# Two-block attention on one core: the second block's exponentials taken for two heads at once, and one head's maxima over two chunks from the positive part of their difference

## The chip, the cores and the metric

The kernel runs on one core of a Trainium2 chip. The metric is device time in microseconds (us): the median of 3 runs is 1816.2 us, between 1811.39 and 1816.44. The trace that is read below is of one profiled execution of 1817.04 us, of which the recorded span of instructions takes 1815.3 us. The engines go by their names in the profile: PE is TensorE (PEld its loading of weights), DVE is VectorE, ACT is ScalarE, POOL is GpSimd, SP issues DMAs.

## What is computed

Two attention blocks, A and B, each with its own input of 2048 tokens by 512 features, 32 heads of 16 features, and its own output; the outputs stand side by side in the result. Block A has a sliding window of 256 tokens, block B is full attention, and it is block B that the change touches.

```python
def _B_ref(x, wqkv, wo):
    B, S, D = x.shape
    H = 32
    Dh = D // H
    qkv = transpose((x @ wqkv).reshape(B, S, 3, H, Dh), 2, 0, 3, 1, 4)
    q, k, v = qkv[0], qkv[1], qkv[2]
    scores = jnp.einsum("bhqd,bhkd->bhqk", q, k) * (Dh ** -0.5)
    p = _softmax(scores, axis=-1)
    o = jnp.einsum("bhqk,bhkd->bhqd", p, v)
    return transpose(o, 0, 2, 1, 3).reshape(B, S, D) @ wo
```

## The kernel before, in words

**Units and steps.** Heads go in groups of four (HG) and queries in chunks of 512 (QC). A unit is one group and one query chunk, so block B has 32 units. Within a unit, 16 steps run over the tiles of 128 keys. One step is, for its 128 keys and the unit's 512 queries: four score matmuls, one per head (`scores`, line 615; 51 rows of K as weights, Q as moving data), an exponential of each 128x512 result (line 622, ScalarE, PSUM to the SBUF tile `p`), and four products of values and exponentials (`weigh2`, line 646), which are issued two steps after their scores and accumulate in PSUM bank 0. A head's 16 features appear as 48 rows, since numbers are split into two parts; 3 further rows carry the negated row maximum, so the exponential sees scores with the maximum already taken off. The heads of a group sit at array rows 0 and 64 (`ROW`): two matmuls that stand next to each other with different halves run in the array at the same time. Here such a couple is called a pair.

**Maxima one unit ahead.** While a unit's steps run, the row maxima of the next unit are made: for each of four tiles of 128 queries and each of four chunks of 512 keys (16 items a unit), the four heads' scores are computed again the other way round (`max2`, line 458; Q as weights, K as moving data), and VectorE reduces them over the keys (line 462) into `mt`. GpSimd then joins the four chunks (`max_chunk`), and splits the result (`max_finish`). PE transposes it (`max_rows`, line 582), ScalarE copies it out, and two DMAs lay it into the 3 rows of Q.

**The order.** Engines work through their instructions in the order in which the code records them, and a semaphore holds an instruction until its data is there or its buffer is free. For block B the order is a string of letters that is walked through again and again. One walk is called a round here: it covers two steps and two items of maxima. Before, with `s` a score matmul and its exponential, `M` the maxima of heads 0 and 1 (one reduction over 128x1024), `m` that of one further head (a reduction over 128x512), and a digit so many quarters of a step's `weigh2`:

```python
ORDER = "ssm4mssMs2msms2sM"
```

The last 20 steps, for which no maxima are left, go by `LAST`, with six matmuls of the output projection after every second step. Eight times early in block B, two output projections of block A (24 matmuls) are put in at a `4`. `STEP` is the planner's own clock per step; it sets when loads and later work are put into the order.

**PSUM.** There are eight banks of 128x512 float32. In block B, before: bank 0 for the products, banks 1 to 3 in turn for scores, banks 4 and 5 as the pair that `M` uses, banks 6 and 7 in turn (`room`) for `m`.

Of the kernel before, what the change touches and what calls it, by code (L numbers as in the profile page):

```python
# [20 lines left out]
HG = 4  # L21
# [13 lines left out]
NEG = -1.0e30  # L35
SCALE = DH ** -0.5
AHEAD = 3
STEP = 2.45
PACE = 16 * STEP


ORDER = "ssm4mssMs2msms2sM"
LAST = "ssss4"
AHEADM = 4
QU = 2.4

# [96 lines left out]
def attention_kernel(ctx: ExitStack, tc: tile.TileContext, xT, wqk, wv, wo, out):  # L143
# [79 lines left out]
    def view(bank):  # L223
        pool, n = bank
        if pool == "u":
            return ps_all[:, n + 1]
        first, width = {"e": (1, 1), "o": (0, 1), "p": (4, 2), "s": (6, 1)}[pool]
        n = first + width * n
        return ps_all[:, n] if width == 1 else ps_all[:, n:n + 2]

# [12 lines left out]
    later = mone.bitcast(mybir.dt.uint16)  # L243
    junk = cst.tile([128, 256], BF16, name="junk")
    xt = [cst.tile([128, 2, 4, 2 * HG], F32, name=f"nm{i}") for i in range(2)]
    opk = [cst.tile([128, HG // 2, S], F32R, name=f"opk{i}") for i in range(2)]
    vt = [cst.tile([128, NT, VP + 16 * i], F32, name=f"vt{i}") for i in range(2)]
    vst = [cst.tile([128, H, VW], F32, name=f"vst{i}") for i in range(2)]
# [4 lines left out]
    def constants():  # L253
        make_identity(nc, ident)
        nc.gpsimd.memset(minus, -1.0)
        nc.gpsimd.memset(wmask, 0.0)
        nc.gpsimd.affine_select(out=wmask[:, 128:], in_=wmask[:, 128:], pattern=[[-1, 128]],
                                compare_op=ALU.is_ge, fill=NEG, base=0, channel_multiplier=1)
        nc.gpsimd.memset(mone, 1.0)
        nc.gpsimd.affine_select(out=mone, in_=mone, pattern=[[0, 2], [1, 128]], compare_op=ALU.is_ge,  # L260
                                fill=zero_fill, base=-1, channel_multiplier=-1)
        nc.vector.memset(ps_all[:, 0], 0.0)
        for v in vst:
            nc.gpsimd.memset(v, 1.0)
        for v in xt:
            nc.gpsimd.memset(v, 0.0)
        nc.gpsimd.memset(vt[1][:, :, VP:], 1.0)
# [166 lines left out]
    def maxima(b, g, c):  # L434

        if not b:
            if (b, g, c) not in mt:
                xt.reverse()
                mt[b, g, c] = xt[0]
            return mt[b, g, c].rearrange("p a s (r q) -> p a r q s", q=4)  # L440
        if (b, g, c) not in mt:
            m = sb.tile([128, NQC, HG, 4], F32, name=f"mt_{b}_{g}_{c}",
                        **(dict(tag="mte", bufs=1) if (b, g, c) == (1, 0, 0) else dict(tag="mt", bufs=3)))
            mt[b, g, c] = m.rearrange("p k h q -> p h q k")
        return mt[b, g, c]

# [124 lines left out]
    def max_rows(b, g, c):  # L571
        n = f"{b}_{g}_{c}"
        nm = parts["nm"].bitcast(BF16).rearrange("p a s (n u) -> p a (s n) u", u=2)[:, :, :, 1]
        if slot[0]:

            bank = M.take("e")
            ps = view(bank)
        else:
            bank, ps = room()
        ps = ps.bitcast(BF16)  # L580
        for a in range(2):
            nc.tensor.transpose(ps[32 * a:32 * a + 32, :128], nm[:, a], ident)
        nt = sb.tile([64, 128], F32, name=f"ntr_{n}", tag="ntr")
        op = nc.scalar.activation(nt, ps[:64, :128], AF.Copy)
        t = mark(op, M.run("ACT", 200, M.pe("c", 80)))
        release(bank, t)
        for a in range(2):
            ready["q", b, g, c] = M.dma(12, t)
            nc.sync.dma_start(opq[b, g, c][ROW[a] + KS:ROW[a] + KM].bitcast(F32).rearrange(
                "s r (q t) -> s (r q) t", t=128), nt[32 * a + 8:32 * a + 32])  # L590
# [14 lines left out]
    def scores(b, g, c, kt, j, heads=1, pieces=((),)):  # L605

        n = f"{b}_{g}_{c}_{kt}"
        pr, a0 = divmod(j, 2)
        banks = [M.take("e" if b else "u") for _ in range(heads)]
        ps = [view(bank) for bank in banks]  # L610
        w = QC if b else sum(x[3] for x in pieces)
        for k, col, q0, n1 in [(kt, 0, 0, QC)] if b else pieces:
            for x in range(heads):
                rows = slice(ROW[a0 + x], ROW[a0 + x] + KM)
                nc.tensor.matmul(ps[x][:, col:col + n1], opk2(g)[rows, pr, 128 * k:128 * k + 128],  # L615
                                 opq[b, g, c][rows, pr, q0:q0 + n1], start=True, stop=True)
            t = M.pe("h", 235 if b else 12 + n1 / 2.4, ready["q", b, g, c])
        if a0 == 0:
            pts[b, g, c, kt, pr] = sb.tile([128, 2, QC], F32, name=f"p_{n}_{pr}", tag="p", bufs=2 * AHEAD)
        p = pts[b, g, c, kt, pr]  # L620
        for x in range(heads):
            op = nc.scalar.activation(p[:, a0 + x, :w], ps[x][:, :w], AF.Exp, scale=SCALE)  # L622
            done = mark(op, M.run("ACT", 60 + w / 1.2, t))
            M.release(banks[x], done)
        if b == 0:

            for d, sign, base in ((0, 1, 0), (2, -1, -1)):
                cols = [col // 128 + x for k, col, q0, n1 in pieces for x in range(n1 // 128)
                        if 4 * c + q0 // 128 + x - k == d]
                for x in cols:  # L630
                    v = p[:, :, 128 * x:128 * x + 128]
                    nc.gpsimd.affine_select(out=v, in_=v, pattern=[[0, 2], [sign, 128]], compare_op=ALU.is_ge,  # L632
                                            fill=zero_fill, base=base, channel_multiplier=-sign)
                    done = M.run("Pool", 360, done)
        ready["p", b, g, c, kt] = done

    def weigh2(g, c, kt, q0, q1):

# [109 lines left out]
    def project_out(b, c, qts):  # L748
        banks, ps = {}, {}
        for p in range(NG // 2):  # L750
            for qt in qts:
                if p == 0 and len(qts) == 4 and qt == 1:
                    pass
                elif p == 0 and len(qts) == 4 and qt == 0:
                    ps[0], ps[1], banks[0], banks[1] = ps_all[:, 4], ps_all[:, 5], None, None
# [66 lines left out]
    def room():  # L822

        if slot[0]:
            slot[1] ^= 1
            return None, view(("s", slot[1]))
        b = M.take("u")
        return b, view(b)
# [308 lines left out]

    M.turn = dict(f=0, h=0, c=0)
    M.load = 0
    M.banks["e"] = M.banks["u"][:3]  # L1140
# [4 lines left out]
    ns, nq, nm, half, got = 0, -8, AHEADM, 0, 0  # L1145
    t0 = M.t["PE"]
    half_tile = 0
    rows = []
    while nq < 4 * len(steps):
        if nm == len(mx) and len(M.banks["e"]) == 3:  # L1150

            M.banks["e"] += [M.t["PE"] + 3000] * 2
        for x in ORDER if nm < len(mx) else LAST:
            k = ns // HG
            if x == "s" and k < len(steps):
# [6 lines left out]
                scores(1, *steps[k], ns % HG)  # L1162
                ns += 1
            elif x in "Mm" and nm < len(mx):
                if nm == AHEADM and got == 0:
# [3 lines left out]
                if x == "M":  # L1169
                    h = (0, 1)  # L1170
                    two = view(("p", 0))
                else:
                    h = (2 + half,)
                    half ^= 1
                    two = room()[1][:, None]
                max2(g, c, qt, kc, h, two)
                got += len(h)
                if got == HG:
                    nm += 1
                    got = 0  # L1180
                    if nm % 16 in (14, 15):
                        max_chunk(1, g, c, nm % 16 - 13)
# [63 lines left out]
```

## Time and profile before

| what | value |
|---|---|
| time, median of 3 | 1816.2 us |
| profiled execution, its span | 1817.04 us, 1815.3 us |
| PE busy | 1792.1 us (99% of the span), 15030 instructions |
| DVE busy | 1508.8 us (83%), 2243 instructions |
| ACT busy | 1400.6 us (77%), 2750 instructions |
| POOL busy | 648.4 us (36%), 1334 instructions |
| granted TensorE clock, mean | 0.996 |

A busy PE here isn't a PE at its peak: its matmuls are pipelined and their ends are modelled. Block B's rounds with maxima end with the last reduction at 1724.8 us. From then on VectorE has nearly nothing to do, and the rest of the span is the last unit and the output projection. The views used below are: the windows (busy time of each engine in a stretch), the groups of instructions by line and shape (line, engine, operation, out<-in, shapes and count, then busy us and mean ns of one, then idle time before them), and the timeline (start in us, length in us, engine, line, operation, count, and in brackets how long the engine had been idle and who released it).

### The profile page before, as it was taken

What the parts mean: (1) busy time and instruction counts of PE and PEld (TensorE: products, weight loads), DVE (VectorE), ACT (ScalarE), POOL (GpSimd) and SP (SyncE); (2) the same over time, 40 slices, a digit from 0 to 9 for tenths busy, and PEclk for the clock granted to TensorE, in tenths of its full rate; (3) what the DMA queues carried; (4) which work ended last, traced back from release to release, by engine and by line L of the source; (5) the groups of instructions that cost most, each with busy time, mean ns of one, the idle gap of its engine ahead of it and who ended that gap; (6) DMA issues with size and microseconds to landing.
All of it is one profiled execution on the core that took longest, in us unless ns stands there. A gap on an engine that the chain in (4) does not pass through costs nothing. (4 is left out here: it accounts for less than half of the span.)

```text
span 1815.3 us, 39121 instructions
## 1 busy us (share of the span) xinstructions
PE 1792.1 (99%) x15030; PEld 911.2 (50%) x15030; DVE 1508.8 (83%) x2243; ACT 1400.6 (77%) x2750; POOL 648.4 (36%) x1334
## 2 busy tenths in 40 slices
PE   9999899999999999999999999999999999999998
PEld 7776566767763555444444444444444434443436
DVE  4666676677779776899999999999999999999901
ACT  4366566665568776799999999999999999999983
POOL 0377777755755331033310024320112422022330
PEclk9999999999999999999999999999999999999999
DMA  8756566545572221311300211130031121010012
GB/s 264 208 182 212 186 190 211 179 139 170 181 202 97 77 86 65 83 30 47 65 17 31 56 49 29 29 78 16 16 76 35 29 63 37 17 54 14 25 37 93
DMA packets 129162, 166.80 MB, mean 92 GB/s; under 512 B 23012, under 2 KB 58852, under 8 KB 128964
## 3 DMA queue, kind: packets, MB, share of 16 engines
q1 hardware_dynamic: 128976, 164.31, 30.8%
q8 instruction: 118, 1.93, 0.5%
q14 instruction: 68, 0.56, 0.1%
HBM read 94.49 MB, written 68.19 MB: 90 GB/s over the span
## 5 line engine op out<-in xcount | busy, mean ns | idle before, releaser
L622 ACT ACTIVATE p<-ps_all 128x512 f32<-128x512 f32 x2432 | 1259.4, 597 | 185.5 <-PE ps_all L615 118.5
L462 DVE TENSOR_REDUCE mt<-ps_all 128x2 f32<-128x1024 f32 x1516 | 1195.3, 871 | 66.0 <-PE ps_all L458 59.2
L615 PE MATMUL ps_all<-oq,opk 51*128 51x512 f32 (+2 forms) x2752 | 773.3, 405 | 4.5 <-ACT p L622 2.1
L458 PE MATMUL ps_all<-opk,oq 48*128 48x512 f32 x2016 | 674.0, 438 | 0.2
L646 PE MATMUL ps_all<-p,vt 128*17 128x256 f32 (+1 forms) x6056 | 587.8, 460 | 0.5 <-ACT ou L672 0.5
L615 PEld LDWEIGHTS ps_all<-oq,opk 51*128 51x128 f32 x2752 | 398.0, 185 | 183.4 <-ACT p L622 157.4
L458 PEld LDWEIGHTS ps_all<-opk,oq 48*128 48x128 f32 x2016 | 308.4, 184 | 314.6 <-DVE mt L462 181.4
L632 POOL TENSOR_SCALAR_AFFINE_SELECT p<-p 128x256 f32<-128x256 f32 x480 | 178.9, 407 | 107.4 <-ACT p L622 107.0
L646 PEld LDWEIGHTS ps_all<-p,vt 128*17 128x17 f32 x6056 | 100.7, 95 | 223.4 <-issue 212.8
L532 POOL TENSOR_TENSOR mu<-mt 128x16 f32<-128x16 f32 x31 | 6.8, 220 | 503.9 <-DVE mt L462 503.9
L514 DVE COPY_PREDICATED ps_all<-mone,ps_all 128x256 f32<-128x256 uint16 x224 | 95.3, 425 | 95.3 <-PE ps_all L505 92.7
L515 DVE TENSOR_REDUCE nm<-ps_all 128x2 f32<-128x512 f32 x224 | 155.2, 693 | 7.7
L700 POOL TENSOR_TENSOR rd<-ld,minus 128x32 f32<-128x32 f32 x15 | 81.9, 5458 | 223.1 <-DMA ld<-od 223.1
L212 PE MATMUL ps_all<-x,w 128*128 128x512 f32 x432 | 112.9, 410 | 1.8 <-ACT x L161 1.2
L340 PE MATMUL ps_all<-x,w 64*128 64x512 f32 x672 | 112.8, 392 | 0.0
L661 PE MATMUL ps_all<-p,vt 128*17 128x384 f32 (+2 forms) x1408 | 96.2, 387 | 5.0 <-POOL p L632 5.0
L212 PEld LDWEIGHTS ps_all<-x,w 128*128 128x128 f32 x432 | 80.9, 194 | 27.4 <-issue 3.0
L295 ACT ACTIVATE raw<-ps_all 128x512 f32<-128x512 f32 x56 | 32.4, 597 | 80.3 <-PE ps_all L212 69.8
L212 PE MATMUL ps_all<-w_o,x_o 128*128 128x512 f32 x384 | 92.7, 396 | 1.0 <-ACT ob L765 1.0
L505 PE MATMUL ps_all<-opk,oq 48*128 48x384 f32 (+2 forms) x512 | 90.3, 367 | 2.4 <-DMA oq<-parts 0.6
L212 PEld LDWEIGHTS ps_all<-w_o,x_o 128*128 128x128 f32 x384 | 70.6, 188 | 30.8 <-issue 11.9
L340 PEld LDWEIGHTS ps_all<-x,w 64*128 64x128 f32 x672 | 80.1, 185 | 8.2
(77 smaller groups left out, 942.1 us busy)
## 6 DMA issues: line engine op xcount, KB each, us to landing
parts<-st SPq DMA_DIRECT2D x64, 512.0 KB
oq<-parts SPq DMA_DIRECT2D x128, 128.0 KB
opk<-parts SPq DMA_DIRECT2D x128, 128.0 KB
od<-ou SPq DMA_DIRECT2D x64, 256.0 KB
vd<-vst SPq DMA_DIRECT2D x32, 272.0 KB
oq<-parts SPq DMA_DIRECT2D x128, 64.0 KB
opk<-parts SPq DMA_DIRECT2D x128, 64.0 KB
t<-od SPq DMA_DIRECT2D x32, 256.0 KB
```

The costliest lines, as they stand in the source:

```text
L212: nc.tensor.matmul(ps, l(u), r(v), start=start and k == 0, stop=stop and k == n - 1)
L340: op = nc.tensor.matmul(view(banks[a ^ turn]), l(u)[rows], r(v)[rows], start=turn == q == 0, stop=turn == 1 and q == 11)
L458: nc.tensor.matmul(ps[:, n], q[rows, 128 * qt:128 * qt + 128], k[rows, kc * QC:kc * QC + QC], start=True, stop=True)
L462: op = nc.vector.tensor_reduce(out=m[:, a:a + len(heads), r, qt, kc], in_=ps, axis=AX.X, op=ALU.max)
L505: nc.tensor.matmul(two[:, a, 0:w], opq[b, g, c][rows, r, 128 * qt:128 * qt + 128], opk2(g)[rows, r, t0:t1], start=True, stop=True)
L514: nc.vector.copy_predicated(two[:, :, 256:384], later, two[:, :, 0:128])
L515: op = nc.vector.tensor_reduce(out=m[:, :, r, qt, 0], in_=two[:, :, 128:384], axis=AX.X, op=ALU.max)
L615: nc.tensor.matmul(ps[x][:, col:col + n1], opk2(g)[rows, pr, 128 * k:128 * k + 128], opq[b, g, c][rows, pr, q0:q0 + n1], start=True, stop= ...
L622: op = nc.scalar.activation(p[:, a0 + x, :w], ps[x][:, :w], AF.Exp, scale=SCALE)
L632: nc.gpsimd.affine_select(out=v, in_=v, pattern=[[0, 2], [sign, 128]], compare_op=ALU.is_ge, fill=zero_fill, base=base, channel_multiplier ...
L646: nc.tensor.matmul(o[32 * j:32 * j + VW, q0:q1], vt[(g // 2) % 2][:, kt, vc:vc + VW], pts[1, g, c, kt, j // 2][:, j % 2, q0:q1], start=kt ...
L661: nc.tensor.matmul(o[32 * j:32 * j + VW, q0:q0 + w], vt[(g // 2) % 2][:, kt, vc:vc + VW], pts[b, g, c, m, j // 2][:, j % 2, col:col + w], ...
```

## The change

Block B only; block A and the last projection keep their work, apart from the bank numbers of the latter.

- A score pair (`x` for array half 0, `y` for half 1) fills two banks, and one exponential of 128x1024 is taken when the second is there (`score`, line 656 for the matmul and 664 for the exponential). Two such pairs of banks, 1-2 and 3-4, take turns.
- All maxima now go through single banks, 5 to 7 in turn. Heads 1, 2 and 3 get one matmul and one 128x512 reduction per item, as `m` had (`part_max`, lines 693 and 707; letters `p q r u t v`).
- Head 0's two chunks of a round are joined: `D` computes the scores of the first chunk, `E` adds into the same bank the scores of the second chunk with negated Q (`negated` makes it on GpSimd, once a unit), so that the bank holds first minus second. ScalarE takes the positive part into an SBUF tile (line 700, in the former `vst` buffers). `B` computes the second chunk's scores in another bank, and one VectorE instruction adds the positive part and reduces over the keys (line 703): second + max(first - second, 0) is the larger of the two. In the first two rounds head 0 is still reduced chunk by chunk (`d`, `e`).
- The order, `STEP`, and `LAST` change. `mt` comes from four fixed tiles that start at a very low number, since head 0 leaves two of its four chunk places unwritten.

```diff
-STEP = 2.45
+STEP = 2.35
...
-ORDER = "ssm4mssMs2msms2sM"
-LAST = "ssss4"
+ORDER = "xyuyx4DpEyxqxyrt4Bv"
+LAST = "xyxy4"
+HALF = {"p": (1, 0), "q": (1, 1), "r": (2, 0), "u": (2, 1), "t": (3, 0), "v": (3, 1), "d": (0, 0), "e": (0, 1)}
...
-        first, width = {"e": (1, 1), "o": (0, 1), "p": (4, 2), "s": (6, 1)}[pool]
+        first, width = {"e": (1, 2), "o": (0, 1), "s": (5, 1)}[pool]
...
+    def score(g, c, kt, pr, a, started=[]):
+
+        n = f"1_{g}_{c}_{kt}"
+        if not started:
+            started[:] = [M.take("e")]
+        bank, *half = started
+        two = view(bank)
+        rows = slice(ROW[a], ROW[a] + KM)
+        nc.tensor.matmul(two[:, a], opk2(g)[rows, pr, 128 * kt:128 * kt + 128], opq[1, g, c][rows, pr], start=True, stop=True)
+        t = M.pe("h", 118, ready["q", 1, g, c])
+        if not half:
+            started.append(a)
+            return
+        del started[:]
+        p = sb.tile([128, 2, QC], F32, name=f"p_{n}_{pr}", tag="p", bufs=2 * AHEAD)
+        pts[1, g, c, kt, pr] = p
+        nc.scalar.activation(p, two, AF.Exp, scale=SCALE)
...
+    def negated(g, c):
+        minus_q.append(minus_q.pop(0))
+        v = minus_q[-1][0:KS, 0]
+        nc.gpsimd.tensor_scalar(v, opq[1, g, c][0:KS, 0].bitcast(F32), -1.0, None, op0=ALU.mult)
...
+    def part_max(x, g, c, qt, kc, held=[]):
...
+        j, half = HALF.get(x, (0, int(x != "D")))
+        r, a = divmod(j, 2)
+        rows = slice(ROW[a], ROW[a] + KS)
+        if x == "E":
+            ps, q = held.pop(0), nq_of[g, c]
+        else:
+            ps, q = room()[1], opq[1, g, c][rows, r]
+        if x == "D":
+            held.append(ps)
+        nc.tensor.matmul(ps, q[:, 128 * qt:128 * qt + 128], opk2(g)[rows, r, (kc + half) * QC:(kc + half + 1) * QC],
+                         start=x != "E", stop=x != "D")
+        t = M.pe("h", 118, ready_)
+        if x == "D":
+            return
+        if x == "E":
+            rl_of.append(rl_of.pop(0))
+            nc.scalar.activation(rl_of[-1], ps, AF.Relu)
+            ready["relu"] = M.run("ACT", 487, t)
+        elif x == "B":
+            nc.vector.tensor_tensor_reduce(rl_of[-1], ps, rl_of[-1], 1.0, LEAST, ALU.add, ALU.max,
+                                           accum_out=m[:, 0, 0, qt, kc // 2 * 3:kc // 2 * 3 + 1])
+            M.run("DVE", 720, t, ready["relu"])
+        else:
+            nc.vector.tensor_reduce(out=m[:, a:a + 1, r, qt, kc + half], in_=ps[:, None], axis=AX.X, op=ALU.max)
+            M.run("DVE", 598, t)
...
         if slot[0]:
-            slot[1] ^= 1
+            slot[1] = (slot[1] + 1) % 3
             return None, view(("s", slot[1]))
```

How the rounds stand on PE. In the rows, L615 and L656 are scores (out<-Q,K), L458 and L693 maxima (out<-K,Q or K and the negated Q, `minus`), L646 and L719 the products; `x2` is two equal rows in a row, and `DVE_49` and `Activation_49` are the counting semaphores of VectorE and ScalarE. A row that names none was let through by an earlier wait. PE of the kernel before, from one `4` up to the next in the middle of block B:

```order
L646 MATMUL ps_all<-p_2_1_2_0_11245,vt_78 17x512 x2
L646 MATMUL ps_all<-p_2_1_2_1_11258,vt_78 17x512 x2
L458 MATMUL ps_all<-opk_75,oq_2_2_10644 128x512 [waits DVE_49]
L615 MATMUL ps_all<-oq_2_1_10218,opk_75 128x512 [waits Activation_49] x2
L458 MATMUL ps_all<-opk_75,oq_2_2_10644 128x512 [waits DVE_49]
L458 MATMUL ps_all<-opk_75,oq_2_2_10644 128x512
L615 MATMUL ps_all<-oq_2_1_10218,opk_75 128x512 [waits Activation_49]
L646 MATMUL ps_all<-p_2_1_3_0_11266,vt_78 17x256 x2
L646 MATMUL ps_all<-p_2_1_3_1_11279,vt_78 17x256 x2
L458 MATMUL ps_all<-opk_75,oq_2_2_10644 128x512 [waits DVE_49]
```

These are a `4`, a stretch of six half-array matmuls and a `2`. PE of the changed kernel, from one `4` to the next:

```order
L719 MATMUL ps_all<-p_2_1_12_0_11129,vt_82 17x512 x2
L719 MATMUL ps_all<-p_2_1_12_1_11135,vt_82 17x512 x2
L693 MATMUL ps_all<-opk_79,oq_2_3_10745 128x512 [waits DVE_49] x2
L693 MATMUL ps_all<-opk_79,minus_7030 128x512
L656 MATMUL ps_all<-oq_2_1_9957,opk_79 128x512 [waits Activation_49]
L656 MATMUL ps_all<-oq_2_1_9957,opk_79 128x512
L693 MATMUL ps_all<-opk_79,oq_2_3_10745 128x512 [waits DVE_49]
L656 MATMUL ps_all<-oq_2_1_9957,opk_79 128x512 [waits Activation_49]
L656 MATMUL ps_all<-oq_2_1_9957,opk_79 128x512
L693 MATMUL ps_all<-opk_79,oq_2_3_10745 128x512 [waits Activation_49]
L693 MATMUL ps_all<-opk_79,oq_2_3_10745 128x512 [waits DVE_49]
L719 MATMUL ps_all<-p_2_1_13_0_11148,vt_82 17x512 x2
```

The letters of this stretch are `4DpEyxqxyrt4`: ten half-array matmuls stand between two full products, where six or four stood between a `4` and a `2`. The last but two row, `r`, is a maximum that waits for ScalarE. Its bank is the one in which `D` and `E` left their difference three uses earlier, so it waits until the positive part has been read out. ScalarE of the changed kernel, in another unit of block B (L664 exponentials, L700 the positive part):

```order
L700 ACTIVATE vst_84<-ps_all 128x512 [waits DVE_49,PE_49]
L664 ACTIVATE p_3_2_11_0_12973<-ps_all 128x1024 [waits PE_49,Activation_49]
L664 ACTIVATE p_3_2_11_1_12979<-ps_all 128x1024 [waits PE_49,Activation_49]
L664 ACTIVATE p_3_2_12_0_13021<-ps_all 128x1024 [waits PE_49,Activation_49]
L664 ACTIVATE p_3_2_12_1_13027<-ps_all 128x1024 [waits PE_49,Activation_49]
L700 ACTIVATE vst_83<-ps_all 128x512 [waits DVE_49,PE_49]
```

Per round ScalarE had eight exponentials of 128x512, and now has four of 128x1024 and one positive part.

More of the change, by code (lines that the diff above doesn't have):

```diff
@@ L37 @@
 AHEAD = 3
-STEP = 2.45
+STEP = 2.35
 PACE = 16 * STEP
-ORDER = "ssm4mssMs2msms2sM"
-LAST = "ssss4"
+ORDER = "xyuyx4DpEyxqxyrt4Bv"
+LAST = "xyxy4"
+HALF = {"p": (1, 0), "q": (1, 1), "r": (2, 0), "u": (2, 1), "t": (3, 0), "v": (3, 1), "d": (0, 0), "e": (0, 1)}
+FIRST = 2
+LEAST = -3.0e38
 AHEADM = 4
@@ L245, in attention_kernel @@
     xt = [cst.tile([128, 2, 4, 2 * HG], F32, name=f"nm{i}") for i in range(2)]
+    mts = [cst.tile([128, NQC, HG, 4], F32, name=f"mt{i}") for i in range(4)]
     opk = [cst.tile([128, HG // 2, S], F32R, name=f"opk{i}") for i in range(2)]
@@ L264, in constants @@
             nc.gpsimd.memset(v, 1.0)
+        for m in mts:
+            nc.gpsimd.memset(m, LEAST)
         for v in xt:
@@ L441, in maxima @@
         if (b, g, c) not in mt:
-            m = sb.tile([128, NQC, HG, 4], F32, name=f"mt_{b}_{g}_{c}",
-                        **(dict(tag="mte", bufs=1) if (b, g, c) == (1, 0, 0) else dict(tag="mt", bufs=3)))
+            if (g, c) == (0, 0):
+                m = sb.tile([128, NQC, HG, 4], F32, name=f"mt_{b}_{g}_{c}", tag="mte", bufs=1)
+            elif (g, c) == (0, 1):
+                m = mts.pop()
+            else:
+                m = mts.pop(0)
+                mts.append(m)
             mt[b, g, c] = m.rearrange("p k h q -> p h q k")
@@ L576, in max_rows @@
             bank = M.take("e")
-            ps = view(bank)
+            ps = view(bank)[:, 0]
         else:
@@ L635, in scores @@
         ready["p", b, g, c, kt] = done
+    def score(g, c, kt, pr, a, started=[]):
[14 more added lines that the diff above has]
+        nc.scalar.activation(p, two, AF.Exp, scale=SCALE)
+        done = M.run("ACT", 913, t)
+        M.release(bank, done)
+        ready["p", 1, g, c, kt] = done
@@ new lines, in attention_kernel @@
+    nq_of, rl_of, minus_q = {}, [], []
+    def negated(g, c):
+        minus_q.append(minus_q.pop(0))
+        v = minus_q[-1][0:KS, 0]
+        nc.gpsimd.tensor_scalar(v, opq[1, g, c][0:KS, 0].bitcast(F32), -1.0, None, op0=ALU.mult)
+        M.run("Pool", 620)
+        nq_of[g, c] = v
+    def part_max(x, g, c, qt, kc, held=[]):
+        m = maxima(1, g, c).rearrange("p (a r) q k -> p a r q k", a=2)
+        follow(("k", 1, g))
+        follow(("q", 1, g, c))
+        ready_ = loaded(1, g, c)
+        j, half = HALF.get(x, (0, int(x != "D")))
[20 more added lines that the diff above has]
+            M.run("DVE", 720, t, ready["relu"])
+        else:
+            nc.vector.tensor_reduce(out=m[:, a:a + 1, r, qt, kc + half], in_=ps[:, None], axis=AX.X, op=ALU.max)
+            M.run("DVE", 598, t)
@@ L751, in project_out @@
             for qt in qts:
[L752 to L755, printed above, removed]
+                if p == 0 and len(qts) == 4:
+                    ps[qt], banks[qt] = ps_all[:, (5, 6, 7, 4)[qt]], None
                 elif p == 0:
@@ L1139, in attention_kernel @@
     M.load = 0
-    M.banks["e"] = M.banks["u"][:3]
+    M.banks["e"] = [max(M.banks["u"][i:i + 2]) for i in (0, 2)]
     slot[0] = True
@@ L1144, in attention_kernel @@
     mx = [(NA + 1 + i // 16, *units[NA + 1 + i // 16][1:], *divmod(i % 16, NQC)) for i in range(16 * turn)]
-    ns, nq, nm, half, got = 0, -8, AHEADM, 0, 0
+    ns, nq, nm = 0, -8, AHEADM
     t0 = M.t["PE"]
@@ L1148, in attention_kernel @@
     rows = []
+    for i in range(2):
+        rl_of.append(vst[i].rearrange("p h d -> p (h d)")[:, 0:QC])
+        minus_q.append(sb.tile([128, 2, QC], F32R, name=f"minus_{i}", tag="st"))
+    negated(*units[NA + 1][1:])
+    parts_done = ""
     while nq < 4 * len(steps):
-        if nm == len(mx) and len(M.banks["e"]) == 3:
-            M.banks["e"] += [M.t["PE"] + 3000] * 2
         for x in ORDER if nm < len(mx) else LAST:
             k = ns // HG
-            if x == "s" and k < len(steps):
+            if x in "xy" and k < len(steps):
                 if ns % HG == 0:
@@ L1161, in attention_kernel @@
                         pop()
-                scores(1, *steps[k], ns % HG)
+                score(*steps[k], ns % HG // 2, int(x == "y"))
                 ns += 1
-            elif x in "Mm" and nm < len(mx):
-                if nm == AHEADM and got == 0:
+            elif not x.isdigit() and x not in "xy" and nm < len(mx):
+                if nm == AHEADM and not parts_done:
                     for _ in range(FILL):
@@ L1168, in attention_kernel @@
                 u, g, c, qt, kc = mx[nm]
[L1169 to L1182, printed above, removed]
+                if nm < AHEADM + 2 * FIRST:
+                    x = {"D": "d", "E": "", "B": "e"}.get(x, x)
+                    parts_done += "" if x else "E"
+                    if not x:
+                        continue
+                part_max(x, g, c, qt, kc)
+                parts_done += x
+                if nm % 16 == 14 and all(y in parts_done for y in "prt") and x in "prt":
+                    max_chunk(1, g, c, 2)
+                if nm % 16 == 12 and len(parts_done) == 9 and nm + 4 < len(mx):
+                    negated(*mx[nm + 4][1:3])
+                if len(parts_done) == 9:
+                    parts_done = ""
+                    nm += 2
+                    if nm % 16 == 14:
+                        max_chunk(1, g, c, 1)
                     if nm % 16 == 0:
```

## The prediction

> **What bounds the kernel now.** First the windows, to find which engine is full in block B's rounds (columns: PE, PEld, DVE, ACT, POOL busy us with counts, granted clock, DMA share, GB/s). The earlier window, from block A, is used further down.
>
> ```profile
> 200.00:400.00 200.00, 192.07 (x1800) 130.75 (x1800) 133.45 (x323) 125.92 (x254) 144.36 (x289) 0.97 0.56 174
> 1000.00:1200.00 200.00, 200.00 (x1732) 81.26 (x1730) 200.00 (x258) 181.14 (x355) 53.65 (x112) 1.00 0.21 46
> ```
>
> VectorE is never idle between 1000 and 1200 us; ScalarE is idle 9% of the time, GpSimd 73%. PE reads as full, but its ends are modelled, so its room has to be found from starts. Then the groups by shape in a stretch of 400 us (1000 to 1400):
>
> ```profile
> L622 ACT ACTIVATE p<-ps_all 128x512 f32<-128x512 f32 x688 | 357.5, 600 | 37.9 <-PE ps_all L615 19.4 <-PE ps_all L458 9.1
> L462 DVE TENSOR_REDUCE mt<-ps_all 128x1 f32<-128x512 f32 x344 | 220.4, 683 | 0.0
> L462 DVE TENSOR_REDUCE mt<-ps_all 128x2 f32<-128x1024 f32 x172 | 209.7, 1219 | 0.0
> ```
>
> A round has two `M` and four `m`, so 172 and 344 reductions are 86 rounds: 400 / 86 = **4.65 us a round**. The two kinds fill all 400 us without idle time, so VectorE sets this. A double reduction takes 1219 - 683 = 536 ns more than a single one; 344 a + 172 (a + 0.536) = 400 gives a = 0.60 us for a single one back to back (its 683 ns overlap the next) and 1.13 for a double: 4 x 0.60 + 2 x 1.13 = 4.65.
>
> How near PE is, the timeline of PE in the last rounds shows:
>
> ```profile
> 1718.03 0.73 PE L615 MATMUL ps_all<-oq,opk 51*128 51x512 f32 x2
> ...
> 1718.69 0.62 PE L646 MATMUL ps_all<-p,vt 128*17 128x256 f32 x8
> 1719.25 0.50 PE L615 MATMUL ps_all<-oq,opk 51*128 51x512 f32 x1
> ...
> 1720.16 1.05 PE L646 MATMUL ps_all<-p,vt 128*17 128x512 f32 x8
> 1721.14 0.50 PE L458 MATMUL ps_all<-opk,oq 48*128 48x512 f32 x1
> ```
>
> Four half-array matmuls take 0.66 us to the start of the products, six 0.91; a `2` 0.56, a `4` 0.98. A round had stretches of 6, 6 and 4 with a `4` and two `2`: 2 x 0.91 + 0.66 + 0.98 + 2 x 0.56 = 4.58. So PE was only 0.07 under VectorE: **VectorE sets the pace, and PE stands just behind.** Inside a stretch:
>
> ```profile
> 1202.06 0.50 PE L615 MATMUL ps_all<-oq,opk 51*128 51x512 f32 x1
> ...
> 1202.40 0.40 PE L615 MATMUL ps_all<-oq,opk 51*128 51x512 f32 x1
> ...
> 1202.63 0.40 PE L615 MATMUL ps_all<-oq,opk 51*128 51x512 f32 x1
> ```
>
> The second pair comes 0.34 after the first, a later one 0.23. The first takes 0.50 instead of 0.40, since its weights are loaded first: 0.10. From the last pair to the products is 0.91 - 0.34 - 0.23 = 0.34.
>
> **The change part by part.** *VectorE*: six single reductions, 6 x 0.60 = 3.60, and the joined one of head 0, which this trace has only narrower and in block A:
>
> ```profile
> L510 DVE CUSTOM_DVE_ANT_0 junk<-ps_all,wmask 128x256 bf16<-128x256 f32 x32 | 13.6, 425 | 16.0 <-PE ps_all L505 12.6 <-DVE nm L510 0.6
> L510 DVE CUSTOM_DVE_ANT_0 junk<-ps_all,wmask 128x128 bf16<-128x128 f32 x32 | 9.3, 291 | 17.4 <-PE ps_all L505 14.9
> 36.99 0.42 DVE L510 CUSTOM_DVE_ANT_0 junk<-ps_all,wmask 128x256 bf16<-128x256 f32 x1
> ...
> 37.57 0.42 DVE L510 CUSTOM_DVE_ANT_0 junk<-ps_all,wmask 128x256 bf16<-128x256 f32 x1
> ```
>
> From start to start 0.58 with 256 elements, and (425 - 291) / 128 = 1.05 ns for each more: 0.85 at 512, the upper end. The lower end is a plain reduction, 0.60. So VectorE needs 4.20 to 4.45 a round; I take 4.45, the nearest row of its kind. Either way it no longer sets the pace if something else takes longer.
>
> *ScalarE*: four exponentials of 1024 and one positive part. Rows of other widths, and a run of five:
>
> ```profile
> L622 ACT ACTIVATE p<-ps_all 128x384 f32<-128x384 f32 x32 | 13.9, 499 | 5.0 <-PE ps_all L615 5.0
> L622 ACT ACTIVATE p<-ps_all 128x256 f32<-128x256 f32 x32 | 10.3, 387 | 3.3 <-PE ps_all L615 1.8 <-POOL p L632 1.0 <-PE ps_all L340 0.5
> 1724.47 2.56 ACT L622 ACTIVATE p<-ps_all 128x512 f32<-128x512 f32 x5
> ```
>
> Back to back one of 512 takes (2.56 - 0.60) / 4 = 0.49, and 512 elements more cost 2 x (600 - 387) = 0.43: 0.92 for 1024, at most 2 x 0.49 = 0.98. The round costs 4 x 0.92 + 0.49 = 4.17, at most 4.41, and the positive part is 0.60 long by the exponential's row.
>
> *PE*: 17 half-array matmuls instead of 16, in two stretches (`DpEyxqxyrt` and `Bvxyuyx`) instead of three, and two `4`. Ten take 0.91 + 2 x 0.23 = 1.37, seven 1.14 (four pairs' time, since four of them use half 0): 1.37 + 1.14 + 2 x 0.98 = **4.47 without waits**. So far every engine is below 4.65.
>
> *The added wait.* `r` takes the bank of `D` and `E`, and waits until ScalarE has read it; behind `r` on PE stand `t`, a `4`, `B` and the next scores, so everything waits with it. What the wait lasts follows from E's start to ScalarE's start, ScalarE's length, and ScalarE's end to PE's start. The first of these links: the pair of 1202.06 above ends at 1202.56, and ScalarE starts 0.04 later:
>
> ```profile
> 1202.60 0.60 ACT L622 ACTIVATE p<-ps_all 128x512 f32<-128x512 f32 x1
> ```
>
> The last: the run of ScalarE that starts at 1724.47 has its first end at 1725.07, and PE, held by it, loads weights 0.05 later:
>
> ```profile
> 1725.12 0.18 PEld L615 LDWEIGHTS ps_all<-oq,opk 51*128 51x128 f32 x1 [0.54 <-ACT p L622]
> ```
>
> Now walk one round from `D`. 0: `D p`. 0.34: `E y`. 0.74: E ends. 0.78: ScalarE takes the positive part (its exponentials are done by then: the scores of the second come at 3.64 of the round before, end 0.40 later, and wait for the first exponential; both are through at about 0.5). 1.38: it ends. 1.43: PE loads weights for `r`, 1.53: `r t` run. Unhindered they would run at 0.34 + 3 x 0.23 = 1.03. **The wait costs 0.50 us a round**, since three pair places (0.69) stand against 0.40 + 0.04 + 0.60 + 0.05 + 0.10 = 1.19. 1.87: the `4`. 2.85: `B v`. 3.19, 3.42, 3.65: `x y`, `u y`, `x`. 3.99: the second `4`. 4.97: `D` again. By the sum, 4.47 + 0.50 = 4.97; with the third decimals of the rows lost, I take **4.95**. No second wait comes on top. `y` of the second couple (3.42) needs the fourth exponential: positive part from 0.78 (0.49 to the next start), two of 0.92 from 1.27, end near 3.2. `u` needs `t` reduced, `D` needs `B`: VectorE has half a microsecond of slack a round. E's negated Q is made a round ahead, on an engine that is 73% idle.
>
> So the round grows by 4.95 - 4.65 = 0.30. Rounds: 31 units of 16 items less the 4 made earlier are 492, two a round: 246, the first two without the difference. 244 x 0.30 = **+73 us**.
>
> *The transposes* of the maxima (once a unit) were hidden, as the round of 4.65 held over 400 us that contain them. PE now has no such cover, because the chain runs through it:
>
> ```profile
> 1206.73 0.23 PE L582 MATMUL ps_all<-ident,nm 128*32 128x128 bf16 x2
> 1206.89 0.50 PE L615 MATMUL ps_all<-oq,opk 51*128 51x512 f32 x1
> ```
>
> 0.16 each, 30 times: **+5**, at least 0. They take a whole score pair now; the pair is free by then (its exponential ends at about 2.3 of the round).
>
> *The last 20 steps*, without maxima:
>
> ```profile
> 1742.34 1.65 PE L212 MATMUL ps_all<-w_o,x_o 128*128 128x512 f32 x6
> ...
> 1747.55 1.65 PE L212 MATMUL ps_all<-w_o,x_o 128*128 128x512 f32 x6
> ```
>
> Two steps with six projection matmuls take 5.21 us. They had five score banks and now have two pairs. After the projection, the first two exponentials end at 0.54 + 2 x 0.92 + 0.1 = 2.5; the second couple of the next step needs that, its products start at 2.9, and with them, the projection (1.6) and 0.98 the two steps take 5.5: ten times 0.3, **+3**, between 0 and 5. The 16 inserted projections are the same matmuls at the same place: nothing. The rows that `negated` and the tiles' start add lie on GpSimd: nothing, and its rival is below.
>
> **A rule against the change.** In the windows above PE was idle 4% of the earlier one and the granted clock was 0.97; in the rounds it was 1.00. The Trainium skill, "TensorE: Matmul & The Clock Gate", section "A second HAM failure mode: psum-queue depth-cycling", says that small idle times between groups of matmuls that cycle through PSUM banks can let the clock fall back again and again. This trace has no such stalls in block B, so it can't decide; by that rule the matmuls would also slow down, and without it the sum stands.
>
> **The rivals.**
> 1. *The wait does not exist in time*: the positive part is out before PE comes to `r`. Then PE's 4.47 holds and the round shrinks by 0.18: 1817.0 - 244 x 0.18 + 8 = **1781**, faster. For it: ScalarE is below its limit, three pairs stand between. Against: 1.19 stands against 0.69, each link from a row. It decides at a positive part that is out within 0.69 us of E's start; the new round equals the old where the wait costs 0.18.
> 2. *The wait is partly paid by shorter turns*: weights for `r` loaded before the bank is free, and turns between half and full array that shrink when PE stood still. Up to 0.3 of the 0.50 could go: round 4.65 to 4.70, **1825 to 1837**, or with a little more nothing measurable. Against: PEld in the row above waited too.
> 3. *GpSimd comes late with the negated Q.* Before it can stand a power of 5.46 us and a normalisation:
>
> ```profile
> L700 POOL TENSOR_TENSOR rd<-ld,minus 128x32 f32<-128x32 f32 x15 | 81.9, 5458 | 223.1 <-DMA ld<-od 223.1
> ```
>
> Some 9 us against a lead of about 8 (a round, and 3 us up to E): up to 2 us in at most 15 units, 30 on top: **1928**.
> 4. *The clock falls in the stalls.* At the 0.97 of block A's window, 4.47 of PE's work becomes 4.61: 244 x 0.14 = 34 on top, **1932**. The Trainium skill's section above is the one that would have it so.
>
> **How the numbers follow.** The forecast: 1817.0 (the profiled execution, 0.8 above the median of the runs shown) + 73 + 5 + 3 = **1898**, chance 0.74. Its own range: the wait from 0.40 (no weight load in it) to 0.60 (ScalarE late by the dearer exponentials) is 24 us either way, with the small terms 1869 to 1925. Rival 1 has 0.12, rival 2 0.06, rival 3 0.05, rival 4 0.03. The range reaches down towards rival 2 and up to 3 and 4: 1845 to 1930, with rival 1 and the ends left out. About 0.3% is what a measurement of this kernel can tell from no change: faster 0.12 (rival 1), same 0.04 (of rival 2), slower 0.84.
>
> **What would show it.** In the changed profile: rounds of 4.95 us; before `r` (line 693) a wait of PE for ScalarE's line 700 of about half a microsecond a round; VectorE idle some 10% in the rounds and ScalarE too; stretches of PE that are as long as worked out but for that wait. Rounds near 4.47 with PE not waiting on line 700 would make it wrong at that step; a full VectorE would show that the joined reduction is dearer than its upper end; waits of `E` for GpSimd speak for rival 3, a clock below 1.00 for rival 4.

## The result and the profile after

The changed kernel takes 1896.14 us (median of 4 runs, 1893.07 to 1898.95) against 1816.32 us before (4 runs, 1811.39 to 1819.41): 1.0437 times as long, 95% interval 1.0405 to 1.0469. The profiled execution took 1898.95 us, 81.9 more than the one of before.

The windows view of the changed kernel shows what became of the full VectorE (PE, PEld, DVE, ACT, POOL busy us with counts, granted clock, DMA share, GB/s):

```profile
1000.00:1200.00 200.00, 192.29 (x1343) 74.97 (x1340) 180.53 (x323) 179.32 (x213) 51.48 (x108) 1.00 0.15 40
```

VectorE is idle 10% of the time, and ScalarE as well. No engine is full, and the kernel is slower. The groups by shape for 1000 to 1400 us, with mean ns of one ahead of the second bar and idle time before them behind it:

```profile
L664 ACT ACTIVATE p<-ps_all 128x1024 f32<-128x1024 f32 x323 | 312.9, 1023 | 34.3 <-PE ps_all L656 33.5 <-PE ps_all L693 0.8
L707 DVE TENSOR_REDUCE mt<-ps_all 128x1 f32<-128x512 f32 x485 | 312.2, 685 | 19.8 <-PE ps_all L693 3.5 <-POOL mg L546 1.8
...
L703 DVE CUSTOM_DVE_ANT_0 vst<-ps_all,vst 128x512 f32<-128x512 f32 x81 | 56.1, 692 | 19.3 <-PE ps_all L693 19.3
L700 ACT ACTIVATE vst<-ps_all 128x512 f32<-128x512 f32 x81 | 48.4, 598 | 7.6
```

One positive part a round: 81 rounds in 400 us, 4.94 us each, where there were 86 of 4.65. The work itself got cheaper, as meant: an exponential of 1024 is 1023 ns long where two of 512 were 1200, and the joined reduction (692 ns) costs as much as a plain one. The timeline of PE shows where the round is lost:

```profile
1202.42 0.50 PE L693 MATMUL ps_all<-opk,oq 48*128 48x512 f32 x2
1202.75 0.39 PE L693 MATMUL ps_all<-opk,minus 48*128 48x512 f32 x1
...
1203.21 0.43 PE L656 MATMUL ps_all<-oq,opk 51*128 51x512 f32 x2
1203.83 0.50 PE L693 MATMUL ps_all<-opk,oq 48*128 48x512 f32 x2 [0.19 <-ACT vst L700]
1204.25 1.05 PE L719 MATMUL ps_all<-p,vt 128*17 128x512 f32 x8
1205.24 0.50 PE L693 MATMUL ps_all<-opk,oq 48*128 48x512 f32 x2
...
1206.37 1.05 PE L719 MATMUL ps_all<-p,vt 128*17 128x512 f32 x8
1207.35 0.50 PE L693 MATMUL ps_all<-opk,oq 48*128 48x512 f32 x2
```

From `D p` (1202.42) to the next `D p` (1207.35) is 4.93 us. The row of 1203.83 is `r t`. Line 700 is named as what released it, and the two stand 0.62 behind the score pair of 1203.21, where an unhindered pair follows in 0.23. ScalarE at the same place:

```profile
1203.17 0.60 ACT L700 ACTIVATE vst<-ps_all 128x512 f32<-128x512 f32 x1
1203.67 1.93 ACT L664 ACTIVATE p<-ps_all 128x1024 f32<-128x1024 f32 x2
1206.07 1.94 ACT L664 ACTIVATE p<-ps_all 128x1024 f32<-128x1024 f32 x2 [0.47 <-PE ps_all L656]
```

The positive part ends at 1203.77, and PE loads weights for `r` 0.05 later:

```profile
1203.82 0.19 PEld L693 LDWEIGHTS ps_all<-opk,oq 48*128 48x128 f32 x2 [0.50 <-ACT vst L700]
```

That the wait is the rule and not one case, the waits from 1000 to 1400 us say (in total us, times, longest):

```profile
PEld ps_all L693 <- ACT vst L700: 40.8, 81, 0.5
...
PE ps_all L693 <- ACT vst L700: 15.3, 80, 0.2
```

81 waits in 81 rounds. PEld's total counts its whole idle time before each, PE's only what the modelled ends leave; neither is the price. The price is what the stretch is longer: 1.83 here, and 1.35 where the wait is absent (the second run with five banks, below), so 0.48 us a round.

### The profile page after: what moved, and what is told of

The parts are those of the page before. It is cut to its first block, busy times and chain, and to the rows that moved or that the text cites. A ratio compares the mean times of both kernels' runs of the same rounds, so it can differ in the third digit from the quotient of the medians.

```text
span 1897.2 us, 37119 instructions
## 1 busy us (share of the span) xinstructions
PE 1825.4 (96%) x13314; PEld 905.5 (48%) x13314; DVE 1464.0 (77%) x2735; ACT 1453.6 (77%) x1970; POOL 695.8 (37%) x1369
## 5 line engine op out<-in xcount | busy, mean ns | idle before, releaser
L664 ACT ACTIVATE p<-ps_all 128x1024 f32<-128x1024 f32 x1024 | 991.1, 1023 | 115.8 <-PE ps_all L656 111.6
L707 DVE TENSOR_REDUCE mt<-ps_all 128x1 f32<-128x512 f32 x1480 | 951.9, 685 | 83.0 <-PE ps_all L693 35.9
L693 PE MATMUL ps_all<-opk,oq 48*128 48x512 f32 x1968 | 568.4, 472 | 46.1 <-ACT vst L700 45.2
L719 PE MATMUL ps_all<-p,vt 128*17 128x512 f32 x4096 | 539.6, 599 | 0.0
L693 PEld LDWEIGHTS ps_all<-opk,oq 48*128 48x128 f32 x1968 | 229.0, 183 | 564.9 <-DVE mt L707 432.4
L656 PE MATMUL ps_all<-oq,opk 51*128 51x512 f32 x2048 | 453.1, 403 | 4.4 <-ACT p L664 3.7
L656 PEld LDWEIGHTS ps_all<-oq,opk 51*128 51x128 f32 x2048 | 264.7, 185 | 54.1 <-ACT p L664 26.5
L633 ACT ACTIVATE p<-ps_all 128x512 f32<-128x512 f32 (+2 forms) x384 | 196.2, 575 | 71.6 <-PE ps_all L626 59.4
L703 DVE CUSTOM_DVE_ANT_0 vst<-ps_all,vst 128x512 f32<-128x512 f32 x244 | 168.8, 692 | 88.0 <-PE ps_all L693 87.8
L773 POOL TENSOR_TENSOR rd<-ld,minus 128x32 f32<-128x32 f32 x15 | 81.9, 5459 | 235.2 <-DMA ld<-od 235.2
L700 ACT ACTIVATE vst<-ps_all 128x512 f32<-128x512 f32 x244 | 145.8, 598 | 24.4 <-PE ps_all L693 2.2
L719 PEld LDWEIGHTS ps_all<-p,vt 128*17 128x17 f32 x4096 | 68.2, 95 | 156.1 <-issue 144.5
L693 PE MATMUL ps_all<-opk,minus 48*128 48x512 f32 x244 | 95.0, 389 | 0.0
```

The source lines that it names most:

```text
L656: nc.tensor.matmul(two[:, a], opk2(g)[rows, pr, 128 * kt:128 * kt + 128], opq[1, g, c][rows, pr], start=True, stop=True)
L664: nc.scalar.activation(p, two, AF.Exp, scale=SCALE)
L693: nc.tensor.matmul(ps, q[:, 128 * qt:128 * qt + 128], opk2(g)[rows, r, (kc + half) * QC:(kc + half + 1) * QC], start=x != "E", stop=x != "D")
L700: nc.scalar.activation(rl_of[-1], ps, AF.Relu)
L703: nc.vector.tensor_tensor_reduce(rl_of[-1], ps, rl_of[-1], 1.0, LEAST, ALU.add, ALU.max, accum_out=m[:, 0, 0, qt, kc // 2 * 3:kc // 2 * 3 ...
L707: nc.vector.tensor_reduce(out=m[:, a:a + 1, r, qt, kc + half], in_=ps[:, None], axis=AX.X, op=ALU.max)
```

## Experiments

The question is whether the reuse of the difference's bank sets the round, and what stands behind it. All eight runs change the kernel after the change; each time stands beside runs of the kernel before on the same chip. "A" is the theory of the prediction, with what is next once the wait is gone.

**The positive part made shorter.** It is taken of 256 of the 512 columns; the other half is left out.

```diff
-            nc.scalar.activation(rl_of[-1], ps, AF.Relu)
+            nc.scalar.activation(rl_of[-1][:, 0:256], ps[:, 0:256], AF.Relu)
```

> ScalarE takes the positive part of the first 256 of the 512 columns only; the other half is left out. Theory A (r waits for line 700; right behind it t waits for p's reduction): the positive part is 0.21 us shorter, so r could go 0.21 earlier, but t's bank is p's of the same stretch, whose reduction ends at about 1.22 us after D, so t runs at 1.37 instead of 1.53: round 4.93 - 0.14 = 4.80, time 1896 - 244 x 0.13 = 1864. Theory B (the wait for line 700 alone): round 4.72, 1845. Theory C (the wait of r is not what lengthens the round): 4.93, 1896.

1868.9 us, 1.0281 times the kernel before (1.0251 to 1.0311). Its timeline of PE, from `D p` to `D p`:

```profile
1205.04 0.50 PE L693 MATMUL ps_all<-opk,oq 48*128 48x512 f32 x2
...
1206.24 0.61 PE L693 MATMUL ps_all<-opk,oq 48*128 48x512 f32 x2
1206.79 1.05 PE L719 MATMUL ps_all<-p,vt 128*17 128x512 f32 x8
...
1209.89 0.50 PE L693 MATMUL ps_all<-opk,oq 48*128 48x512 f32 x2
```

`r` starts 1.20 after `D`, against 1.41, so 0.21 earlier as the shorter positive part allows. But the products start only 0.08 earlier (1.75 against 1.83), since the couple `r t` takes 0.61 instead of 0.50 here: `t` is held. VectorE shows by whom, in the reductions of `p` and then `q`:

```profile
1205.61 1.29 DVE L707 TENSOR_REDUCE mt<-ps_all 128x1 f32<-128x512 f32 x2 [0.25 <-PE ps_all L693]
```

The first of the two, of `p`, ends at 1206.30, and the weights of `t` are loaded from 1206.36. The median round over the 243 distances between two `E` is 4.84 (4.94 before the edit). Theory A's 4.80 is 0.04 off, B's 0.12. So the length of the positive part goes into the round, but a second wait, that of `t`, stands right behind.

**The positive part taken twice.**

```diff
             nc.scalar.activation(rl_of[-1], ps, AF.Relu)
+            nc.scalar.activation(rl_of[-1], ps, AF.Relu)
```

> The positive part is taken twice, one after the other. Theory A (line 700 stands in the chain that sets the round): one more instruction of ScalarE back to back, 0.49 us, goes into the round in full: 5.43, time 1896 + 244 x 0.49 = 2016. Theory C (ScalarE, idle some 10% of a round, has room for it, or another wait sets the round): less than 0.2 a round, below 1945.

2050.7 us, 1.1281 (1.1248 to 1.1314). ScalarE:

```profile
1206.19 0.60 ACT L700 ACTIVATE vst<-ps_all 128x512 f32<-128x512 f32 x1
1206.82 0.60 ACT L701 ACTIVATE vst<-ps_all 128x512 f32<-128x512 f32 x1
```

The second starts 0.63 after the first, not the 0.49 that A had: it starts 0.03 after the first's end. Both write the same tile, which is the likely reason, though no run tests it. 0.63 x 244 = 154 on top of 1896 is 2050. The whole of it appears in the time although ScalarE has 10% to spare. That rules out C: idle time on an engine is no room for work that stands in the chain.

**More banks for the maxima.** Score matmuls of array half 1 are left out, and an exponential reads the bank of half 0 twice. A score pair then needs one bank. The matmuls left out ran beside others, so that PE's own time stays. With four banks:

```diff
-        first, width = {"e": (1, 2), "o": (0, 1), "s": (5, 1)}[pool]
+        first, width = {"e": (1, 1), "o": (0, 1), "s": (4, 1)}[pool]
...
-        two = view(bank)
+        two = view(bank)[:, None].to_broadcast([128, 2, QC])
...
-        nc.tensor.matmul(two[:, a], opk2(g)[rows, pr, 128 * kt:128 * kt + 128], opq[1, g, c][rows, pr], start=True, stop=True)
+        if a == 0:
+            nc.tensor.matmul(view(bank), opk2(g)[rows, pr, 128 * kt:128 * kt + 128], opq[1, g, c][rows, pr], start=True, stop=True)
...
-            slot[1] = (slot[1] + 1) % 3
+            slot[1] = (slot[1] + 1) % 4
```

> The score matmuls of array half 1 are left out, and each exponential reads the bank of half 0 twice, so a pair needs one bank and the maxima get four in turn instead of three. The matmuls of half 1 run beside those of half 0, so PE loses no time by it. Theory A (the bank of the difference is reused too early): the fourth use after D is t, which stands in the same pair place as r, so t now waits for line 700 and the round stays at 4.93: 1896. Theory B (three banks are simply few, and each one more shortens the waits): t's wait for p and r's for the difference both ease, round 4.80 or less, 1864 or below.

1895.5 us, 1.0428 (1.0350 to 1.0505; the two executions lie at 1889.9 and 1901.1), and no change against the 1896.1 of three banks. The median round is 4.95, against 4.94. The stretch after `D`, and the wait in it:

```profile
1202.45 0.50 PE L694 MATMUL ps_all<-opk,oq 48*128 48x512 f32 x2
...
1203.46 0.88 PE L694 MATMUL ps_all<-opk,oq 48*128 48x512 f32 x2
1204.28 1.05 PE L720 MATMUL ps_all<-p,vt 128*17 128x512 f32 x8
PEld ps_all L694 <- ACT vst L701: 34.1, 81, 0.4
```

`r` is on time now (1.01 after `D`), but `t` in the same row ends late, and the products start 1.83 after `D` as they did. The positive part (line 701 here) is still waited for once in every round, now by `t`. A fourth bank alone buys nothing, as A had it, and B's 1864 is missed. The run also shows that leaving out half of the scores does not by itself shorten the round. The edit for five banks is the same with `"s": (3, 1)` and `% 5`.

> As with four banks, the scores of half 1 left out, but the maxima get five banks in turn. Theory A: the fifth use after D is B, behind the products, 1.3 us later: the wait for line 700 is gone. What comes next is the second score couple of a round, which waits for the fourth exponential (ends 3.22 us after D, wanted at 3.15 less 0.15): round 4.68, time 1896 - 244 x 0.25 = 1835. Theory D (nothing stands behind that wait): PE's own 4.47, 1784. Theory C (the bank is not the cause): 4.93, 1896.

1828.3 us, 1.0059 (1.0034 to 1.0085). The wait for line 700 is gone. What stands there now:

```profile
1201.76 0.50 PE L694 MATMUL ps_all<-opk,oq 48*128 48x512 f32 x2
...
1202.66 0.50 PE L657 MATMUL ps_all<-oq,opk 51*128 51x512 f32 x1
1203.09 1.05 PE L720 MATMUL ps_all<-p,vt 128*17 128x512 f32 x8
...
1205.41 1.05 PE L720 MATMUL ps_all<-p,vt 128*17 128x512 f32 x8
1206.39 0.50 PE L694 MATMUL ps_all<-opk,oq 48*128 48x512 f32 x2
```

The stretch `Bvxux` takes 1.33 (1201.76 to 1203.09) instead of 1.13, as its second score is held, and the waits say by whom:

```profile
PEld ps_all L657 <- ACT p L665: 35.5, 95, 0.6
```

That is the exponential two back. (Two larger rows of that view, of line 694 for VectorE, 72.3, and for ScalarE, 62.9, stand in the next run too, at 74.8 and 66.3, where no stretch is longer for them.) The median round is 4.65, by chance that of the kernel before; 4.68 was expected. The same with the shorter positive part:

> Five banks for the maxima with the scores of array half 1 left out, and the positive part of only 256 of 512 columns. Theory A (behind the wait for line 700 stands the chain second score couple, products, E, positive part, exponentials three and four): the positive part is 0.21 shorter in that chain, so the round falls from 4.65 to PE's own 4.46, time 1828 - 244 x 0.19 = 1782, below the kernel before. Theory D (the 4.65 of five banks is another limit, such as ScalarE's sum or VectorE's): ScalarE's sum falls by 0.21 too, but it was at 4.17, and VectorE's at 4.26, so the round would stay near 4.65: 1828.

1794.4 us, 0.9875 (0.9809 to 0.9941). The round is 4.46 in the median, and every stretch now has PE's own length:

```profile
1202.06 0.50 PE L694 MATMUL ps_all<-opk,oq 48*128 48x512 f32 x2
...
1203.41 1.05 PE L720 MATMUL ps_all<-p,vt 128*17 128x512 f32 x8
1204.39 0.49 PE L694 MATMUL ps_all<-opk,oq 48*128 48x512 f32 x2
...
1205.52 1.05 PE L720 MATMUL ps_all<-p,vt 128*17 128x512 f32 x8
1206.50 0.50 PE L694 MATMUL ps_all<-opk,oq 48*128 48x512 f32 x2
```

1.35 and 1.13 with two products of 0.98 are 4.44. This is what the change could give if nothing waited; it leaves out half of the scores and is no version to use. The total is 12 us above the 1782 expected. In the profiled execution, which took 1798.0 us where the other took 1790.8, the granted clock (third number from the end) was 0.50 from 564 to 587 us,

```profile
564.00:587.00 23.00, 23.00 (x87) 8.20 (x84) 13.55 (x24) 13.38 (x16) 6.14 (x7) 0.50 0.23 70
```

and four rounds there take 6.1 to 8.1, together 12 us more than at the median. What holds the other execution above 1782 stays open. The rounds with the transposes are no reason: they are 0.46 longer than the others here, and 0.46 in the five-bank run on which the 1782 stands.

**Without the difference.** Head 0 reduced chunk by chunk throughout, `FIRST = 1000` and `STEP = 2.45`:

> Head 0's maxima are reduced chunk by chunk in all rounds (no difference, no positive part, no joined reduction), with the exponentials of two heads and three banks kept; STEP 2.45 as before, which is the planner's clock. Theory A (three banks in turn make each matmul wait for the reduction of the third one before it): r waits for d's reduction and runs at 1.37 instead of 1.03, t waits for p's and runs at 1.98; round 5.41, time 1816 + 246 x 0.76 = 2003. Theory B (without the positive part only VectorE's sum is left): 8 x 0.61 = 4.86, 1816 + 246 x 0.21 = 1868.

2002.5 us, 1.102 (1.0969 to 1.1072), as A has it to within 1 us. From `d p` to `d p`, and the wait of the maxima for VectorE from 1000 to 1400 us:

```profile
1204.89 0.50 PE L693 MATMUL ps_all<-opk,oq 48*128 48x512 f32 x2
...
1206.17 1.10 PE L693 MATMUL ps_all<-opk,oq 48*128 48x512 f32 x2
1207.20 1.05 PE L719 MATMUL ps_all<-p,vt 128*17 128x512 f32 x8
...
1210.28 0.49 PE L693 MATMUL ps_all<-opk,oq 48*128 48x512 f32 x2
PEld ps_all L693 <- DVE mt L707: 180.8, 296, 0.9
```

A round of 5.39, its long stretch 2.31, with `r t` taking 1.10. The reductions of `d` and `p` end at 1206.12 and 1206.72, and the weights of `r` and `t` are loaded 0.05 after each. So leaving the difference out does not help: with the wide exponentials, this order and three banks the kernel is slower still. It does not say that the difference costs nothing; its length goes into the round, as the runs above show. VectorE's sum of 8 x 0.61 = 4.86 is not the limit either.

**Another order.** `ORDER = "xy2xyqDEry2pxyxtB4vu"`, all work done:

> The changed kernel with another order, xy2xyqDEry2pxyxtB4vu: a 2 and two further score matmuls between E and the reuse of its bank. Theory A: the positive part is covered by products, no wait for line 700 is left, but a third stretch costs PE 0.32 a round more than two, and PE's own sum is 4.79: 1896 - 244 x 0.15 = 1860, still above the kernel before. Theory B (with three banks some wait for VectorE takes the place of the one removed): 4.93 or more, 1896 or more.

1889.7 us, 1.0399 (1.0349 to 1.0450): the expected 1860 was missed. Six of eight rounds of a unit take 4.81, close to the 4.79 expected. The other two take 5.29 and 5.36. In these PE waits for ScalarE twice a unit, at the score pair after the transposes and where the products of a new unit need bank 0:

```profile
1124.23 0.51 PE L656 MATMUL ps_all<-oq,opk 51*128 51x512 f32 x2 [0.16 <-ACT p L664]
...
1134.84 0.63 PE L719 MATMUL ps_all<-p,vt 128*17 128x256 f32 x8 [0.49 <-ACT ou L745]
```

Neither was counted; at 0.48 and 0.55 us in each of 30 units they make up the 30 us missing. So this order moves the wait, and the third stretch takes back most of what it saves.

**The difference alone.** Exponentials of one head, three score banks, four banks for maxima, `ORDER = "x2yx2uyvxpDEy4yBrtxq"`. The main edit, beside the banks and `% 4`:

```diff
-        nc.scalar.activation(p, two, AF.Exp, scale=SCALE)
+        nc.scalar.activation(pts[1, g, c, kt, pr][:, a], ps, AF.Exp, scale=SCALE)
```

> The difference alone: exponentials of one head as before, scores in three single banks, maxima in four, order x2yx2uyvxpDEy4yBrtxq. Theory A: PE has three stretches again, 4.79 without waits, ScalarE needs 9 x 0.49 = 4.41, VectorE 4.26; if no wait adds, 4.79: 1816 + 244 x 0.14 = 1850. Theory B (three single banks for eight exponentials, and the positive part between them, make PE wait for ScalarE): 5 or more, above 1900. Theory C (VectorE's saving comes through where the pairs of banks are not taken): below 4.65, below 1816.

1954.3 us, 1.0755 (1.0701 to 1.0809), a miss. The median round is 4.87 (A: 4.79), but one round in eight takes 6.5: PE comes to the transposes before GpSimd has the maxima,

```profile
1113.78 0.23 PE L593 MATMUL ps_all<-ident,nm 128*32 128x128 bf16 x2 [1.38 <-POOL nm L570]
```

1.6 us a unit and 50 us in all. Of the 104 us above A's 1850, another 20 are the longer median, and 13 stand behind the last reduction (104.0 us to the end, against 90.5 in the kernel before). The rest, some 20, goes with the clock: after 7 of these 30 waits the granted clock fell to half, for 3.4 to 6.8 us each, 44 us in all, which by an estimate (half of that time lost) is up to 22 us. One such stretch:

```profile
779.00:785.00 6.00, 6.00 (x32) 2.13 (x30) 3.32 (x6) 3.62 (x7) 0.00 (x0) 0.50 0.01 4
```

So the time lies where theory B had it, but hardly by B's wait: all idle time of PE from 550 to 1800 us is put down to GpSimd, and the longer median leaves B 20 us at most. This run says little of the difference without wide exponentials: its order adds a wait of its own. Whether a better order would bring that half of the change below the kernel before stays open. No full version faster than the kernel before was found.

## Why the prediction was right

1898 us were predicted, 1896.1 came. The steps, one by one:

- **What bounded the kernel before**: VectorE at 4.65 a round, PE 0.07 behind. VectorE then fell to 6 x 0.61 + 0.62 = 4.28 of 4.94 us, and the time did not fall with it.
- **The walk of one round**: `E` at 0.34 (measured 0.33 after `D`), positive part at 0.78 (0.75), weights for `r` at 1.43 (1.40), first products at 1.87 (1.83), `B` at 2.85 (2.82), second products at 3.99 (3.95), next `D` at 4.95 to 4.97 (4.93). The wait was taken at 0.50 and cost 0.48. Each link came from a row of before, none of them from the kernel's own run.
- **The sum**: the round grew by 0.29, not 0.30: 244 x 0.286 (4.936, the median, less 4.65) = 70 against 73. The round with transposes is 5.12, so 0.19 more than the others; 30 of them make 6 against 5. The last part, from the last reduction (1724.8 before, 1801.8 after) to the end, grew by 4.9 against 3; two steps there now take 5.6 to 5.7, expected 5.5. That is 80 of 81.9; the other 2 are not assigned. That the total of 81 came so near is partly luck: the rounds were taken 3 too high, and the small terms 3 too low. The last part's rows:

```profile
1811.21 0.50 PE L656 MATMUL ps_all<-oq,opk 51*128 51x512 f32 x2 [0.42 <-ACT p L664]
...
1812.62 1.66 PE L215 MATMUL ps_all<-w_o,x_o 128*128 128x512 f32 x6
...
1818.32 1.67 PE L215 MATMUL ps_all<-w_o,x_o 128*128 128x512 f32 x6
```

- **A term that was mis-sized**: the joined reduction was taken at 0.85, by rows in which each waits for the one before it; from its start to the next reduction's start it takes 0.62, the lower end. It had no weight in the sum, as VectorE had slack either way.
- **What the prediction did not see**: "No second wait comes on top" holds for the changed kernel as it is, but two more limits stand close behind the one named. With a shorter positive part `t` waits for the reduction of `p` (round 4.84), and with more banks the second score couple waits for the fourth exponential (4.65). Rival 1's 1781 was thus never what a shorter wait alone would have given; only with all three gone (1794, with half of the scores left out) does PE's own time show.
- **The rivals**: 1 fell with the wait in 81 of 81 rounds, and 2 with its price, 0.48 of the 0.50. For 3, no wait of PE for the negated Q is among the waits. For 4, the granted clock was 1.00 from 540 to 1880 us, although each round lost half a microsecond on PE, and PE is idle for 3.9% of that window, the share that it had in block A at 0.97. The rule of the Trainium skill, "TensorE: Matmul & The Clock Gate", section "A second HAM failure mode: psum-queue depth-cycling", did not come into play at idle times of this size.
- **Longer waits**: PE's waits of 1.4 us in the run of the difference alone were followed by a falling clock. So rival 4 is answered for waits of half a microsecond only.

## What to carry to other kernels

Before summing busy times per engine, follow one buffer around: who writes it, who reads it last, and which instruction on an in-order engine asks for it next. An edit that takes work off a full engine, but puts one more reader on a buffer that comes back within a few instructions, can make every engine idle and the kernel slower. When such a wait is found, ask for the next limit behind it as well: here three stood within 0.5 us of a round of 4.9, and adding one bank, or halving the read, each showed only the next.

## What the runs showed of the hardware that was not expected

- Two ScalarE instructions that write the same tile start 0.63 us apart, where others of that size start 0.49 apart: the second starts 0.03 after the end of the first, 0.60 long.
- The joined reduction over 512 elements from PSUM and SBUF (692 ns long) lets the next VectorE reduction start after 0.62 us, in all 243 cases of the changed kernel. Its accumulator's read (83 ns long in the block A rows of before too) starts at the same moment and costs no extra time here.
- Where PE stood still for about 1.4 us in block B's rounds, the granted clock sometimes fell to half within 3 us of the end of the wait: after 7 of 30 such waits in the run of the difference alone, for 3.4 to 6.8 us, and after one of 1.39 us in the second five-bank run, for 24 us. After the wait of 0.5 us that stands in every round of the changed kernel it never did. That the standing still brings the fall is not shown.
